# Pooled attention and a routed FFN: scores by key without row maxima, heads in array tiles, FFN rows by indirect DMA

## The chip, the core and the metric

The kernel runs on one core of one Trainium2 chip. The metric is the device time of one launch in microseconds, lower is better. All data is fp32. The engines are TensorE (PE in the rows; its weight loads are PEld), VectorE (DVE), ScalarE (ACT), GpSimd (POOL) and SyncE (SP), which here only issues DMAs.

## The reference

```python
# attention: q, k, v are (8 batches, 8 heads, 1152, 64)
q_pool = q.reshape(B, H, S // 2, 2, D).mean(axis=3)        # 576 queries
scores = (1 / sqrt(D)) * q_pool @ k.transpose(0, 1, 3, 2)
scores = scores - scores.max(axis=-1, keepdims=True)
attn = exp(scores)
attn = attn / (attn.sum(axis=-1, keepdims=True) + 1e-09)
x = (attn @ v) -> (B, 576, 512)                             # heads side by side
# routed FFN, per batch, on the 128 tokens of highest score x @ w_gate
h = maximum(x[top] @ w1, 0)                                 # w1: 512 x 1024
out = x.copy()
out[top] = x[top] + sigmoid(score[top])[:, None] * (h @ w2) # w2: 1024 x 512
```

q, k and v are random numbers of size 0.1.

## The kernel before

Heads go in pairs, 32 pairs in all. `load_pair` (L112) loads a pair on SP: k with 128 partitions of nine rows of 64 numbers each, q, and v with a column of ones beside it. `prepare_pair` (L140) adds each two queries on GpSimd (L144), transposes k and the pooled q on TensorE in 128x128 blocks (L164, L173) and copies them out of PSUM, so that a head's 64 dimensions lie on 64 partitions, head 0 on the first half and head 1 on the second.

The work then runs in steps of one score tile: 128 queries of one head against all 1152 keys, nine steps a pair (four query tiles per head; the ninth holds the last 64 queries of both heads). `scores` (L182) makes three matmuls of 384 columns (L188), queries as the weights. `exponents` (L197) takes row maxima on VectorE (L200), folds them (L202, L203) and runs three exponents on ScalarE with the maximum as bias (L208). `transposed` (L217) turns the attention tile with nine TensorE transposes (L222) and copies each third out (L227 on ScalarE, L229 on VectorE). `weighted` (L233) multiplies by the values (L241): nine chunks, attention as the weights, 65 moving columns, the last of which collects the row sums. `normalized` (L249) divides and writes x.

`advance` (L485) sets the order: the scores of a step, then the transposes of the step before mixed with the values of the one before that. A generator of the next pair's preparation and one of the last batch's FFN are called once a step in between.

`routed` (L273) is that FFN: gate scores from x (L282), a row of all scores by transposes (L307, L315), ranks by comparison (L332, L341, L351), a 0/1 matrix of token against slot (L368), its transposes (L379, L383), the chosen rows by matmul with that matrix (L394), the two FFN layers (L412, L427), and the update spread over all tokens by matmul (L446) and added (L453). x then goes to the output in one piece. The order of instructions is the framework's, by the order of the program and priorities.

Of the kernel before, what the change touches and what calls it, by code (L numbers as in the profile page):

```python
# [9 lines left out]

P = 128
F32 = mybir.dt.float32
I32 = mybir.dt.int32
AF = mybir.ActivationFunctionType
ALU = mybir.AluOpType
AX = mybir.AxisListType


def _rows_of(ap_1d: bass.AP, parts: int) -> bass.AP:
    """The same row for each of `parts` partitions."""  # L20
    return dataclasses.replace(ap_1d, ap=[[0, parts]] + [list(x) for x in ap_1d.ap])


@with_exitstack
def kernel(
    ctx: ExitStack,
# [9 lines left out]
):  # L36
    """Pooled-query attention, two heads at a time, then the routed FFN of a batch while the next
    batch's attention runs.

    Keys: key p * NC + c is row p of chunk c, so a partition's rows of k and v lie together.  # L40
    Tokens: token p * NF + t is row p of tile t < NF; the last TAIL tokens are tile NF. The last
    tiles of a pair's two heads share one score tile, by queries in a block diagonal.
    """
    nc = tc.nc

    B, H, S, D = q.shape
    Sp = S // 2
    Dm = H * D
    F = moe_w1.shape[1]
    NC = S // P  # L50
    NF = Sp // P
    TAIL = Sp - NF * P
    NT = NF + 1
# [3 lines left out]
    G = 3  # L57
# [3 lines left out]
    D1 = D + 1  # L61
    # The mean of two queries is half their sum.
    scale = 0.5 / math.sqrt(D)
# [8 lines left out]
    const = ctx.enter_context(tc.tile_pool(name="const", bufs=1))  # L72
    load = ctx.enter_context(tc.tile_pool(name="load", bufs=2))
    work = ctx.enter_context(tc.tile_pool(name="work", bufs=3))
    small = ctx.enter_context(tc.tile_pool(name="small", bufs=4))
# [8 lines left out]
    make_identity(nc, ident[:, :])  # L84
    # before[p, j] = 1 where j < p
    before = const.tile([P, P], F32, name="before")
    nc.gpsimd.memset(before[:, :], 1.0)
    nc.gpsimd.affine_select(
        out=before[:, :],
        in_=before[:, :],  # L90
        compare_op=ALU.is_gt,
        fill=0.0,
# [16 lines left out]

# [1 line left out]

    def load_pair(b, hp):  # L112
# [16 lines left out]
        )  # L129
        # The column of ones gives the sums of the attention's rows.  # L130
        v_sb = load.tile([P, 2, NC, D1], F32, name="v_sb", bufs=3)
# [8 lines left out]
    def prepare_pair(pair):  # L140
        """kT and qT: head, then dimension, by key or pooled query; a PSUM tile at a time."""
        qp = load.tile([P, NT, 2, D], F32, name="qp")
# [90 lines left out]
    def weighted(step, g, j, at):  # L233
        """Chunks of group g of attention times values, of head j, into column block `at`."""
        v_sb, t = step["pair"]["v"], step["t"]
        rows = P if t < NF else TAIL
        cols = slice(0, P) if t < NF else slice(j * TAIL, (j + 1) * TAIL)
        if g == 0 and at == 0:
            av_tiles["av"] = ps_av.tile([P, NF, D1], F32, name="av")
        for c in range(g * CG, (g + 1) * CG):  # L240
            nc.tensor.matmul(  # L241
                av_tiles["av"][0:rows, at, :],
                lhsT=step["pT"][:, c, cols],
                rhs=v_sb[:, j, c, :],
                start=(c == 0),
                stop=(c == NC - 1),
            )

    def normalized(step):  # L249
        """The finished column blocks, divided by their rows' sums, into x."""  # L250
        x, j, t, hp = step["x"], step["j"], step["t"], step["pair"]["hp"]
# [18 lines left out]

# [1 line left out]

    def routed(b, x):  # L273
        """The FFN of batch b on its `capacity` best tokens, in units to put between steps."""
        tiles = [(t, P if t < NF else TAIL) for t in range(NT)]

        if slots:
# [14 lines left out]
            gate = ffn.tile([P, NT], F32, name="gate")  # L292
            # exp(88) is finite, and 1 / (1 + exp(88)) is nothing beside 1.
            nc.vector.tensor_scalar(
# [7 lines left out]

            # All scores on every partition, bit for bit, by transposing columns repeated.
            sc_row = ffn.tile([P, Sp], F32, name="sc_row")
# [17 lines left out]

            # rank: how many tokens come before, by score, equal scores by position.
            parts = ffn.tile([P, NT, 3], F32, name="rank_parts")
# [39 lines left out]
        for s0, w in slots:  # L364
            # pick[token, slot] = 1 where the token's rank is the slot.
            pick = ffn.tile([P, NT, P], F32, name="pick")
# [101 lines left out]

    # ---- the steps, each one score tile; a step's transposes and its product with the values
    # ---- come one and two steps later, the next pair and the last batch's FFN in between  # L470

# [13 lines left out]
    def advance(now):  # L485
        """The stages of the step before and of the one before that, after `now`'s scores."""
        if now is not None:
# [42 lines left out]


# [1 line left out]
_INS = ["q", "k", "v", "moe_w_gate", "moe_w1", "moe_w2"]  # L533
# [28 lines left out]
```

## Time and profile before

| | |
|---|---|
| time, median of 3 | 1845.32 us (1843.73 to 1845.55) |
| span of the profiled execution | 1838.1 us |
| TensorE / VectorE / ScalarE / GpSimd busy | 1809.5 / 954.7 / 763.1 / 73.1 us |
| chain that ended last | TensorE 98% |
| mean granted TensorE clock | 0.997 |
| DMA | 166,459 packets, 72.42 MB, 39 GB/s over the span |

How to read it: busy time is the union of an engine's instructions; matmuls are pipelined, so their durations overlap and only their pitch tells what one costs. The chain goes back from the last instruction, at each step to what released it; what is not on it costs nothing by itself.

### The profile page before, as it was taken

How to read it: one execution, taken by the hardware profiler on the slowest of the kernel's cores; microseconds unless marked ns; L12 is line 12 of the kernel's file. 1: busy time of each engine (PE TensorE's matmuls, PEld its weight loads, DVE VectorE, ACT ScalarE, POOL GpSimd, SP SyncE). 2: the span in 40 equal slices, each digit the busy share in tenths (PEclk: the TensorE clock that was granted, in tenths of full speed). 3: DMA queues.
4: the chain of work that ended last, by engine and by line, in shares of the span. 5: the costliest groups of instructions: out<-in, count | busy, mean ns of one | idle time of the engine just before them, and what ended most of it. 6: DMA issues, size and time to landing. Idle time of an engine off the chain costs nothing.

```text
span 1838.1 us, 29462 instructions
## 1 busy us (share of the span) xinstructions
PE 1809.5 (98%) x11648; PEld 1359.5 (74%) x11648; DVE 954.7 (52%) x2609; ACT 763.1 (42%) x1545; POOL 73.1 (4%) x201
## 2 busy tenths in 40 slices
PE   8999999999999999999999999999999999999996
PEld 5777777777778677776778777777777867778674
DVE  2355566445663456535664356644566445663451
ACT  2244444334443344434444344443444434443440
POOL 1000000000000000000000000000000000000000
PEclk9999999999999999999999999999999999999998
DMA  8111111112110111102111111111211101100000
GB/s 213 39 39 40 40 39 28 40 27 65 27 39 27 49 42 40 39 14 65 39 30 36 27 52 40 40 27 27 65 32 34 39 27 53 27 14 1 24 4 26
DMA packets 166459, 72.42 MB, mean 39 GB/s; under 512 B 150832, under 2 KB 154928, under 8 KB 165296
## 3 DMA queue, kind: packets, MB, share of 16 engines
q1 hardware_dynamic: 166320, 70.53, 14.9%
q8 instruction: 92, 1.51, 0.3%
q14 instruction: 47, 0.39, 0.1%
HBM read 61.08 MB, written 9.44 MB: 38 GB/s over the span
## 4 chain that ended last, share of the span: by engine, by line
PE 98%; DVE 1%; DMA 0%; ACT 0%; issue 0%; SPq 0%; POOL 0%
PE sc L188 34%; PE av L241 31%; PE tr L222 19%; PE ps L412 3%; PE ps L427 3%; PE ps L394 3%; PE ps L446 2%; PE tr L164 2%; PE tr L173 1%; PE tr L177 0%; DMA q_sb<-in_q_dram 0%; PE ps L379 0%; DVE x L453 0%; DVE gate_prod L282 0%; PE ps L307 0%; DVE cmp L341 0%
## 5 line engine op out<-in xcount | busy, mean ns | idle before, releaser
L241 PE MATMUL av<-v_sb,pT 128*128 128x65 f32 (+1 forms) x5760 | 700.9, 261 | 1.0 <-DVE x L264 1.0
L200 DVE TENSOR_REDUCE top<-sc 128x1 f32<-128x384 f32 x864 | 481.2, 557 | 404.3 <-PE sc L188 358.8
L241 PEld LDWEIGHTS av<-v_sb,pT 128*128 128x128 f32 (+1 forms) x5760 | 662.0, 183 | 25.5 <-issue 24.4
L188 PE MATMUL sc<-kT,qT 64*128 64x384 f32 (+1 forms) x1728 | 656.2, 512 | 1.7 <-ACT p L208 1.3
L227 ACT COPY pT<-tr 128x384 f32<-128x384 f32 x576 | 275.4, 478 | 897.5 <-PE tr L222 894.7
L208 ACT ACTIVATE p<-sc,neg 128x384 f32<-128x384 f32 x864 | 467.9, 581 | 39.8 <-DVE neg L203 22.5
L188 PEld LDWEIGHTS sc<-kT,qT 64*128 64x128 f32 (+1 forms) x1728 | 306.2, 191 | 222.2 <-issue 60.4
L222 PE MATMUL tr<-ident,p 128*128 128x128 f32 x2592 | 452.7, 284 | 0.0
L222 PEld LDWEIGHTS tr<-ident,p 128*128 128x128 f32 x2592 | 305.4, 154 | 159.2 <-issue 144.9
L229 DVE COPY pT<-tr 128x384 f32<-128x384 f32 x288 | 160.6, 558 | 133.9 <-PE tr L222 130.8
L167 DVE COPY kT<-tr 128x384 f32<-128x384 f32 x96 | 53.5, 558 | 88.2 <-PE tr L164 88.1
L144 POOL TENSOR_TENSOR qp<-q_sb 128x256 f32<-128x256 f32 x64 | 45.0, 724 | 1024.1 <-PE tr L177 764.5
L255 DVE TENSOR_SCALAR rec<-av 128x4 f32<-128x4 f32 (+1 forms) x96 | 15.2, 159 | 108.5 <-PE av L241 108.5
L453 DVE SCALAR_TENSOR_TENSOR x<-ps,gate,x 128x512 f32<-128x512 f32 (+1 forms) x40 | 30.0, 749 | 68.0 <-PE ps L446 67.5
L412 PE MATMUL ps<-xeT,w 128*128 128x128 f32 x512 | 63.7, 278 | 1.4 <-ACT hT L421 0.7
L412 PEld LDWEIGHTS ps<-xeT,w 128*128 128x128 f32 x512 | 59.5, 192 | 2.2 <-ACT hT L421 0.9
L427 PE MATMUL ps<-w,hT 128*128 128x512 f32 x128 | 57.5, 593 | 0.7 <-ACT hT L421 0.7
L202 DVE TENSOR_REDUCE neg<-top 128x1 f32<-128x3 f32 x288 | 44.5, 155 | 23.5 <-ACT pT L227 1.4
L164 PE MATMUL tr<-ident,k_sb 128*128 128x128 f32 x288 | 49.6, 284 | 6.5 <-DMA k_sb<-in_k_dram 6.5
L394 PE MATMUL ps<-pick,x 128*128 128x128 f32 (+1 forms) x320 | 50.5, 300 | 0.3 <-ACT pickT L386 0.3
L203 DVE TENSOR_SCALAR neg<-neg 128x1 f32<-128x1 f32 x288 | 43.9, 153 | 8.6 <-DVE neg L202 0.2
L394 PEld LDWEIGHTS ps<-pick,x 128*128 128x128 f32 (+1 forms) x320 | 41.9, 196 | 7.1 <-ACT pickT L386 0.5
(59 smaller groups left out, 447.4 us busy)
## 6 DMA issues: line engine op xcount, KB each, us to landing
k_sb<-in_k_dram SPq DMA_DIRECT2D x64, 288.0 KB, 3.9
v_sb<-in_v_dram SPq DMA_DIRECT2D x64, 288.0 KB, 3.7
q_sb<-in_q_dram SPq DMA_DIRECT2D x32, 512.0 KB, 3.9
out_dram<-x SPq DMA_DIRECT2D x8, 1024.0 KB, 3.9
w<-in_moe_w_dram SPq DMA_DIRECT2D x2, 2048.0 KB, 13.3
q_tail<-in_q_dram SPq DMA_DIRECT2D x32, 64.0 KB, 3.7
out_dram<-x SPq DMA_DIRECT2D x8, 128.0 KB, 2.7
w_gate<-in_moe_w_gate_dram SPq DMA_DIRECT2D x1, 256.0 KB, 7.2
```

Of the source, the lines that this page charges most:

```text
L164: nc.tensor.transpose(tr[:, i * P : (i + 1) * P], pair["k"][:, g * CG + i, :, :], ident[:, :])
L167: nc.vector.tensor_copy(kT[:, g * CG : (g + 1) * CG, :].rearrange("p c n -> p (c n)"), tr[:, 0 : CG * P])
L188: nc.tensor.matmul(sc[:, :], lhsT=pair["qT"][rows, t, :], rhs=pair["kT"][rows, g * CG : (g + 1) * CG, :].rearrange("p c n -> p (c n)"), st ...
L200: nc.vector.tensor_reduce(top[:, g : g + 1], step["sc"][g][:, :], AX.X, ALU.max)
L208: nc.scalar.activation(p[:, g * CG : (g + 1) * CG, :].rearrange("p c n -> p (c n)"), step["sc"][g][:, :], AF.Exp, bias=neg[:, 0:1], scale= ...
L222: nc.tensor.transpose(tr[:, i * P : (i + 1) * P], step["p"][:, g * CG + i, :], ident[:, :])
L227: nc.scalar.copy(to, tr[:, 0 : CG * P])
L229: nc.vector.tensor_copy(to, tr[:, 0 : CG * P])
L241: nc.tensor.matmul(av_tiles["av"][0:rows, at, :], lhsT=step["pT"][:, c, cols], rhs=v_sb[:, j, c, :], start=(c == 0), stop=(c == NC - 1),)
L394: nc.tensor.matmul(pv[:, c, 0:w], lhsT=x[0:rows, t, c * P : (c + 1) * P], rhs=pick[0:rows, t, 0:w], start=(t == 0), stop=(t == NT - 1),)
L412: nc.tensor.matmul(pv[:, f, 0:w], lhsT=w1[:, c, (f0 + f) * P : (f0 + f + 1) * P], rhs=xeT[:, c, 0:w], start=(c == 0), stop=(c == ND - 1),)
L427: nc.tensor.matmul(ps[0:w, 0:Dm], lhsT=hT[:, f, 0:w], rhs=w2[:, f, :], start=(f == 0), stop=(f == NFC - 1),)
```

## The change

The old code stays whole as `_any_scores`, behind a branch at the end of the program (comments are dropped). A new class `_Plain` runs first:

- k and q are loaded by 32-column halves of a head, so that a partition holds a 32x32 block's row (pieces of 128 bytes in DRAM); VectorE transposes the blocks (`prepare_pair`). No transposes of k and q on TensorE.
- Scores are made with keys as the weights and 288 pooled queries (half of the 576) as moving columns, for both heads: head 0 on array rows 0 to 63, head 1 on 64 to 127, into two PSUM banks. ScalarE takes one exponent over both, without a maximum.
- The result is already attention by key, so it is the moving operand of attention times values; v of a head is the weights, 64 columns, head 0 into output partitions 0 to 63 and head 1 into 64 to 127 of one bank.
- Row sums: attention tiles are added up on VectorE, then summed over keys by a matmul with ones (`normalized`). All sums are kept, and the number outside 0.05 to 1e12 is counted at the end (`outside`); if it is not zero, the old code runs after all.
- x is written to a DRAM buffer in pieces of 128 bytes (`finished`); the FFN copies the buffer to the output, finds ranks as before, gathers the 128 chosen rows by an indirect DMA, and writes their results over the output's rows by another.
- The order of instructions is that of the program (`manual_schedule`). A step is a group of three key chunks of a half; six steps a pair. The FFN's units come in two steps out of three.

```diff
+    def load_pair(self, b, hp):
+        kb = self.load.tile([P, self.KB, BLK], F32, name="kb")
+        qb = self.load.tile([P, self.QB, 2, BLK], F32, name="qb")
+        v_sb = self.load.tile([P, 2, self.NC, self.D], F32, name="v_sb", bufs=3)
+        for j, ds, rows in self.quarters():
+            h = 2 * hp + j
+            nc.sync.dma_start(
+                kb[rows, :, :], self.k[b, h, :, ds].rearrange("(n i) d -> i n d", i=BLK)
+            )
+            nc.sync.dma_start(
+                qb[rows, :, :, :].rearrange("i n r d -> i (n r) d"),
+                self.q[b, h, :, ds].rearrange("(i m) d -> i m d", i=BLK),
+            )
...
+    def prepare_pair(self, pair):
+        nc.gpsimd.tensor_tensor(
+            out=qp[:, :, :], in0=pair["q"][:, :, 0, :], in1=pair["q"][:, :, 1, :], op=ALU.add
+        )
...
+        nc.vector.transpose(pair["kT"][:, :], pair["k"].rearrange("p n d -> p (n d)"))
+        nc.vector.transpose(pair["qT"][:, :], qp.rearrange("p n d -> p (n d)"))
+
+    def scores(self, grp):
...
+        for u in range(G):
+            c = grp["g"] * G + u
+            sc = self.ps_sc.tile([P, 2, 512], F32, name="sc")
+            for j in range(2):
+                rows = slice(j * self.D, (j + 1) * self.D)
+                nc.tensor.matmul(
+                    sc[:, j, 0:n],
+                    lhsT=pair["kT"][rows, c * P : (c + 1) * P],
+                    rhs=pair["qT"][rows, qs],
...
+            nc.scalar.activation(grp["p"][:, u, :, :], sc[:, :, 0:n], AF.Exp, scale=self.scale)
+
+    def weighted(self, grp):
+        if grp["g"] == 0:
+            self.av = self.ps_av.tile([P, 512], F32, name="av")
+        for u in range(G):
+            c = grp["g"] * G + u
+            for j in range(2):
+                nc.tensor.matmul(
+                    self.av[j * self.D : (j + 1) * self.D, 0:n],
+                    lhsT=grp["pair"]["v"][:, j, c, :],
+                    rhs=grp["p"][:, u, j, :],
+                    start=(c == 0),
+                    stop=(c == self.NC - 1),
+                )
...
+    def added(self, grp, half):
...
+        nc.vector.tensor_tensor(
+            out=acc[:, :, :],
+            in0=first[:, :, :],
+            in1=grp["p"].rearrange("p u j n -> p u (j n)"),
+            op=ALU.add,
+        )
...
+    def drained(self, half):
+        self.nc.vector.transpose(
+            half["avb"].rearrange("p n d -> p (n d)"), self.av[:, 0 : self.HALF]
+        )
+
+    def normalized(self, half):
...
+            nc.tensor.matmul(
+                ps[j * self.D : (j + 1) * self.D, 0:n],
+                lhsT=self.ones[:, 0 : self.D],
+                rhs=half["sum"][:, j, :],
...
+        nc.vector.transpose(smb.rearrange("p n d -> p (n d)"), ps[:, 0:n])
+
+    def finished(self, half):
...
+            nc.sync.dma_start(
+                half["xs"][:, d0 + ds.start : d0 + ds.stop].rearrange("(i n) d -> i n d", i=BLK),
+                x[rows, hp, :, :],
+            )
+    def routed(self, b, xs, part):
...
+        nc.sync.dma_start(self.out[b], xs[:, :])
...
+            nc.gpsimd.indirect_dma_start(
+                out=xe[0:w, :],
+                in_=xs[:, :],
+                in_offset=bass.IndirectOffsetOnAxis(ap=index[0:w, 0:1], axis=0),
...
+            nc.gpsimd.indirect_dma_start(
+                out=rows_out,
+                out_offset=bass.IndirectOffsetOnAxis(ap=index[0:w, 1:2], axis=0),
+                in_=xe[0:w, :],
+    def run(self):
...
+        for step in range(n_groups + 2):
...
+                self.scores(groups[step])
+            if 1 <= step <= n_groups:
+                self.weighted(groups[step - 1])
+            if step < n_groups:
+                self.added(groups[step], halves[step // self.NG])
+            if step >= 1 and step % self.NG == 0:
+                self.drained(halves[step // self.NG - 1])
+            if step >= self.NG + 1 and step % self.NG == 1:
+                half = halves[step // self.NG - 1]
+                self.normalized(half)
+                if half["s"] == 1:
+                    self.finished(half)
...
+            else:
+                next(routing, None)
+            if step < n_groups and i == 3 and n + 1 < len(pairs):
+                self.prepare_pair(upcoming)
...
+        with tc.manual_schedule():
+            outside = plain.run()
+    with tc.If(outside > 0):
+        _any_scores(tc, *args)
```

`quarters` gives the two heads' two 32-column halves, each with its 32 partitions. In PSUM, score tiles have three buffers of two banks, `av` one bank, and all other TensorE outputs (the sums and the FFN's) one.

## Rows read from the trace of the kernel before

**Rows 1.** The page, busy us, share of the span and instructions of each engine.

```profile
PE 1809.5 (98%) x11648; PEld 1359.5 (74%) x11648; DVE 954.7 (52%) x2609; ACT 763.1 (42%) x1545; POOL 73.1 (4%) x201
```

**Rows 2.** The page, chain that ended last: shares by engine, then by line.

```profile
PE 98%; DVE 1%; DMA 0%; ACT 0%; issue 0%; SPq 0%; POOL 0%
PE sc L188 34%; PE av L241 31%; PE tr L222 19%; PE ps L412 3%; PE ps L427 3%; PE ps L394 3%; PE ps L446 2%; PE tr L164 2%; PE tr L173 1%; PE tr L177 0%; DMA q_sb<-in_q_dram 0%; PE ps L379 0%; DVE x L453 0%; DVE gate_prod L282 0%; PE ps L307 0%; DVE cmp L341 0%
```

**Rows 3.** Groups by form: line, engine, op, tile, shape, count | busy us, mean ns | idle before.

```profile
L188 PE MATMUL sc<-kT,qT 64*128 64x384 f32 x1536 | 584.9, 513 | 1.7 <-ACT p L208 1.3 <-ACT qT L174 0.4
L188 PE MATMUL sc<-kT,qT 128*128 128x384 f32 x192 | 71.3, 509 | 0.0
L200 DVE TENSOR_REDUCE top<-sc 128x1 f32<-128x384 f32 x864 | 481.2, 557 | 404.3 <-PE sc L188 358.8
L222 PE MATMUL tr<-ident,p 128*128 128x128 f32 x2592 | 452.7, 284 | 0.0
L227 ACT COPY pT<-tr 128x384 f32<-128x384 f32 x576 | 275.4, 478 | 897.5 <-PE tr L222 894.7
```

**Rows 4.** Timeline, two stretches: start us, us, engine, line, op, count [idle before <-releaser].

```profile
102.69 1.48 PEld L241 LDWEIGHTS av<-v_sb,pT 128*64 128x64 f32 x24 [0.17 <-issue]
...
845.16 2.10 PE L188 MATMUL sc<-kT,qT 128*128 128x384 f32 x6
847.10 0.49 PE L222 MATMUL tr<-ident,p 128*128 128x128 f32 x3
848.40 1.05 ACT L208 ACTIVATE p<-sc,neg 128x384 f32<-128x384 f32 x2 [0.24 <-DVE neg L203]
849.94 1.08 PE L446 MATMUL ps<-ye,pickT 128*128 128x512 f32 x2
850.95 2.20 PE L188 MATMUL sc<-kT,qT 64*128 64x384 f32 x6
853.08 0.55 PE L222 MATMUL tr<-ident,p 128*128 128x128 f32 x3
```

**Rows 5.** Timeline of the last FFN: w1 units (L412) and w2 (L427).

```profile
1807.90 3.84 PE L412 MATMUL ps<-xeT,w 128*128 128x128 f32 x32 [0.68 <-ACT xeT L403]
...
1816.95 7.13 PE L427 MATMUL ps<-w,hT 128*128 128x512 f32 x16 [0.69 <-ACT hT L421]
```

**Rows 6.** Groups by form, as rows 3: ScalarE copies, VectorE comparisons, GpSimd's add.

```profile
L174 ACT COPY qT<-tr 128x512 f32<-128x512 f32 x32 | 18.7, 585 | 14.4 <-PE tr L173 14.3
L341 DVE TENSOR_SCALAR_CACHE_REDUCE cmp<-sc_row,gate_sc 128x576 f32<-128x576 f32 x8 | 6.4, 805 | 0.0
L341 DVE TENSOR_SCALAR_CACHE_REDUCE cmp<-sc_row,gate_sc 128x192 f32<-128x192 f32 x8 | 3.2, 404 | 0.0
L144 POOL TENSOR_TENSOR qp<-q_sb 128x256 f32<-128x256 f32 x64 | 45.0, 724 | 1024.1 <-PE tr L177 764.5 <-PE ps L315 231.2 <-DMA q_sb<-in_q_dram 28.4
```

**Rows 7.** The page's packets and one issue; a window: length, busy by engine, clock, DMA share, GB/s.

```profile
DMA packets 166459, 72.42 MB, mean 39 GB/s; under 512 B 150832, under 2 KB 154928, under 8 KB 165296
...
k_sb<-in_k_dram SPq DMA_DIRECT2D x64, 288.0 KB, 3.9
...
610.00:611.00 1.00, 1.00 (x3) 0.38 (x2) 0.00 (x0) 0.00 (x0) 0.00 (x0) 1.00 1.04 237
```

**Rows 8.** Timeline of TensorE early on, and a window there (clock: third number from the end).

```profile
11.48 5.49 PE L188 MATMUL sc<-kT,qT 64*128 64x384 f32 x8 [0.38 <-ACT qT L174]
...
55.32 4.21 PE L188 MATMUL sc<-kT,qT 64*128 64x384 f32 x6
...
86.43 3.81 PE L188 MATMUL sc<-kT,qT 128*128 128x384 f32 x6
93.02 2.20 PE L188 MATMUL sc<-kT,qT 64*128 64x384 f32 x6
...
55.00:60.00 5.00, 5.00 (x11) 2.38 (x10) 2.11 (x4) 0.00 (x0) 0.00 (x0) 1.00 0.00 0
```

**Rows 9.** A window of the tail, columns as in rows 7.

```profile
1780.00:1838.10 58.10, 38.48 (x231) 27.38 (x229) 17.25 (x64) 7.51 (x16) 0.00 (x0) 0.91 0.05 21
```

More of the change, by code (lines that the diff above doesn't have):

```diff
@@ L11 @@
 P = 128
+BLK = 32
+G = 3
 F32 = mybir.dt.float32
@@ L24, with _any_scores @@
 @with_exitstack
-def kernel(
+def _any_scores(
     ctx: ExitStack,
@@ new lines, with kernel @@
+@with_exitstack
+def kernel(
+    ctx: ExitStack,
+    tc: tile.TileContext,
+    q: bass.AP,
+    k: bass.AP,
+    v: bass.AP,
+    moe_w_gate: bass.AP,
+    moe_w1: bass.AP,
+    moe_w2: bass.AP,
+    capacity: int,
+    out: bass.AP,
+):
+    args = (q, k, v, moe_w_gate, moe_w1, moe_w2, capacity, out)
+    if capacity % P == 1:
+        _any_scores(tc, *args)
+        return
+    with ExitStack() as stack:
+        plain = _Plain(stack, tc, *args)
+        with tc.manual_schedule():
+            outside = plain.run()
+    with tc.If(outside > 0):
+        _any_scores(tc, *args)
```

401 lines of the change are left out of this document (added).

## The prediction

> **What bounds the kernel now.** I read the busy table first [rows 1]: TensorE has work for 1809.5 of 1838.1 us, VectorE for 954.7, ScalarE for 763.1, GpSimd for 73.1. "Busy" alone proves little, so the chain of waits comes next [rows 2]: 98% of the chain that ended last lies on TensorE, and its three large shares are the score matmuls (L188, 34%), attention times values (L241, 31%) and the transposes of attention (L222, 19%). So time falls only with TensorE's work, until another engine or the DMA is late.
>
> The groups by form [rows 3] give that work. A matmul here is two passes, each with its own weight load: 864 score tiles stand as 1536 + 192 passes. A 64-row pass of 384 columns takes as long as a 128-row one (513 and 509 ns with the pipeline's ends): half the rows idle is not half the time. The timeline [rows 4] gives the pitch behind these means. At 845.16 six 128-row score passes start and the next transposes follow at 847.10: 1.94 / 6 = 0.323 us per 384 columns, 0.84 ns a column.
>
> **What the change removes.** All 2592 transposes of attention, the row maxima (481.2 us of VectorE), the copies of transposed attention (275.4 us of ScalarE for two groups in three, the third on VectorE) and the transposes of k and q on TensorE [rows 3]; in the routed FFN the pick matmuls (L394) and the scattering ones (L446).
>
> **What TensorE then has.** A pair of heads is six steps (two halves of 288 queries, three groups of three key chunks), 192 steps in all. A step has 3 chunks x 2 heads x 2 passes of scores and as many of attention times values, each of 288 columns: 288 x 0.84 = 0.242 us. A weight load of 128 columns can come every 0.12 us (32 passes in 3.84 [rows 5]), one of 64 columns every 0.06 (24 in 1.48 us [rows 4]), so both hide under 0.242.
>
> One question carries the sum: the two heads of a chunk use different rows of the array (scores, 64x128) or different columns (values, 128x64). Does TensorE run them at the same time?
> - One after the other: 24 x 0.242 = 5.81 us a step.
> - Side by side: passes start in program order (head 0 first, head 0 second, head 1 first, head 1 second), so head 1's first pass runs beside head 0's second, and its second beside the next chunk's first. 12 passes take 7 places instead of 12: 2 x 7 x 0.242 = 3.39 us.
>
> No row of before shows two tiles at once: there every row-tiled score tile of a step is on the same head. The serial rows are nearer in form; yet I take side by side, since within a pair of tiles nothing is shared that the rows show as a cost: other array cells, other input partitions, other output banks or partitions. Both ends stay in the range. The Trainium skill (TensorEngine Tiling (Array Packing), "Tiling Modes") says that different tiles can execute weight loads and matmuls in parallel; no run here shows it, and by it alone a step would be the 3.39 us.
>
> Each step changes tile form twice. That has a price in the timeline [rows 4]: from the start of L446's two passes at 849.94 to the 64-row scores at 850.95 is 1.01 us, where two passes of 512 columns are 0.86, so 0.15 going in; and the six 64-row passes hold the next transposes for 853.08 - 850.95 = 2.13 us instead of 1.94, 0.19 going out. Together 0.34 a step. So a step is 3.73 us, and 192 of them 716 us.
>
> Beside that:
> - the sums of the rows by a matmul with ones, 4 passes in 3 places per half, 0.73 us x 64 = 47 us;
> - the FFN of a batch: two w1 units of 3.84 us, w2 of 7.13 less its end, 6.9 [rows 5]; four transposes of the gathered rows 0.6; the gate scores' row 1.0; columns, index matmuls 1.5; eight units that each change tile form once more, 8 x 0.17 = 1.4; sum 19.1. Seven batches run it between steps: 134 us. The eighth is in the tail.
>
> **Who could be late.** ScalarE: 576 exponents of 576 columns. Two of 384 take 1.05 us [rows 4], and copies of 512 and 384 columns differ by 107 ns [rows 6], 0.84 ns a column, so 0.525 + 192 x 0.00084 = 0.69 us, 395 us in all and 2.1 per step of 3.73: hidden, and the score tiles have three buffers. If TensorE is serial, hidden still more.
>
> VectorE: comparisons of 576 and 192 columns take 805 and 404 ns [rows 6], so 1.04 ns a column and 0.2 fixed. Per pair: four adds of 1728 columns, 2.0 us each; four of 576, 0.81; two drains, two transposes of sums and two products of 288, 0.5 each; small ones 0.64; k and q in 32x32 blocks (1152 and 576 columns) and the gate's reduction, 3.0: 17.9 us. No row shows a 32x32 transpose; I take a column per cycle like the others, with twice that as the bad end (+3.2 us a pair, still under TensorE's 22). Times 32 is 573; the FFN adds about 12 a batch, 667 us in all. Hidden on average. Not always: the one output bank `av` waits for its drain, which stands on VectorE behind the adds and, in some steps, behind a rank unit of 3 us. I charge 20 us, bounds 0 and 100.
>
> GpSimd: an add of 256 columns takes 724 ns [rows 6], so 576 about 1.6 us, two per pair, hidden. The gather and the scatter of rows by indirect DMA have no row; a gather has two empty units (over 7 us) to land, against 3.9 us from issue to landing of a plain load [rows 7], so I charge it only in the tail.
>
> DMA: k and q now come in pieces of 128 bytes, x goes to DRAM in such pieces. Per pair: k 4608, q 4608, v 2304 of 256 bytes, x 2304: 13,824 packets, 442,000 in all against 166,459 now. While the queues were full of 256-byte packets they moved 237 GB/s [rows 7], 0.93 packets per ns. At that rate a pair needs 14.9 us, of about 28 that it lasts. Loads are issued nearly a pair ahead; on SP they stand behind the writes of x and, once a batch, the copy of 1.2 MB to the output, some 10 us. Hidden, until packets come at under half that rate. A page of the Trainium skill speaks against this part: DMA: Bandwidth & Descriptors, "Specifications", asks for at least 512 bytes, below which a transfer reads, modifies and writes. The trace's 256-byte loads show no such loss at 237 GB/s; for stores it shows nothing, and if only the 2304 stores cost double, the pair needs 17.3 us, still hidden.
>
> **Start and tail.** Before, the first scores start at 11.5 us [rows 8]. Now 9216 packets of k and q come first (9.9 us at that rate, with 0.8 to the first issue and 2 to land), then GpSimd's add and the block transposes: 16 us. TensorE's clock starts low: at 55.32 six score passes take 4.21 us, at 93.02 the same six take 2.20 [rows 8], the first at 1.2 GHz, the second at 2.4, though the granted clock is shown as 1.00 there. What came just before was the first step of 128-row scores (86.43); 64-row steps had gone on since 11.5 with TensorE hardly idle. Side by side the array is filled as by those, so I charge 20 us; if it stayed low until the first FFN, about 110.
>
> Tail: from 1780 on before has 58.1 us [rows 9]. The new one has no scattering matmuls, but writes x to DRAM, gathers, and scatters (three transfers of about 4 us), and at the end reads the check's count and branches on every engine. The low clock can come in it as it did (0.91 on the mean of those 58.1 us). I take 68.
>
> Sum: 16 + 20 + 716 + 47 + 134 + 20 + 68 = 1021 us of span. The profiled execution of before, 1838.1, stands 7.2 below the median of 1845.3, so 1028: I say **1030**. Its own range is 900 (no empty places, no stalls) to 1150 (clock late).
>
> **Rivals.**
> - Only one of the two tile kinds runs side by side: five more places of 0.242 per step, 1.21 x 192 = 232 us: 1260. For it: nothing says that rows and columns behave alike.
> - Neither does: 464 + 15 for the sums: 1510, up to 1700 if the clock stays low to the first FFN. For it: every row of before is serial. Against it: as above.
> - The DMA binds: at 40 ns a packet per engine instead of 17, a pair takes 34.6 us, 1110 + 85 for start and tail: 1200. Before's packets speak against it, their size for it.
> - Slower than before: neither kind overlaps and half-filled passes keep the clock at 1.2 GHz, as they did from 11.5 to 86 us. All of TensorE's 1311 us is doubled: 2820. It decides from the point where over a quarter of that work (335 us) runs at the low clock. Against it: 64-row scores in the middle of before did not bring the clock down.
> - The change does not do what it says: a sum outside its bounds sends the whole old code after the new: 2880. q and k are 0.1 in size, so exponents are near 1 and each sum near 1152, within 0.05 and 1e12.
>
> **How the numbers follow.** Side by side 0.62; one kind 0.12; neither 0.12; DMA or VectorE in the way (1150 to 1500) 0.06; slower by the clock 0.07; by the branch 0.01. The range 900 to 1520 takes in the first, the second, most of the DMA case and half of the third: over 0.8. A measurement tells this kernel from no change at about 0.2%. All cases but the last two are faster: 0.91; within 0.2%: 0.01; slower 0.08.
>
> **What would show it.** Score passes of the two heads that start within a few ns of each other in pairs, a step of 3.7 us, VectorE near 65% and DMA packets near 442,000 show the steps right. A step of 5 or 6.2 us shows a rival; score passes 0.48 us apart show the clock; TensorE waiting on v, k or q shows the DMA, and waiting on `av` VectorE.

## The result, and the profile after

The changed kernel takes 951.93 us (median of 4 runs, 951.33 to 953.0) against 1844.53 us for the kernel before (1842.5 to 1845.55): ratio 0.5176, 95% interval 0.5145 to 0.5207. The forecast was 1030 us, so the way was right and the size 8% too high. The profiled execution spans 949.5 us.

The page of the changed kernel: busy us, share of the span and instructions; the granted TensorE clock in 40 slices (tenths of full speed); packets; the chain that ended last.

```profile
PE 844.1 (89%) x5695; PEld 500.2 (53%) x5695; DVE 629.0 (66%) x1069; ACT 359.5 (38%) x625; POOL 109.4 (12%) x91
...
PEclk9999998999999999999999999899998999989958
...
DMA packets 453419, 84.97 MB, mean 89 GB/s; under 512 B 450528, under 2 KB 450528, under 8 KB 453088
...
issue 39%; PE 27%; DVE 18%; SPq 5%; POOL 5%; DMA 4%; ACT 2%; POOLq 0%; DVEq 0%
```

Beside [rows 1] TensorE has fallen from 1809.5 to 844.1 us, and its 98% of the chain [rows 2] has become 27%, with VectorE at 18%: TensorE still has the most work, but it now waits for others too. The 39% of "issue" is time for which this view names no releaser; one piece of it, 24.05 us, stands ahead of GpSimd's product at 474.05, and TensorE was at work in most of it. So these shares are a hint only, and the waits below carry the reading. The clock has 8s in the middle, and 5 and 8 at the end.

The timeline of TensorE in a stretch without disturbance: start us, us, engine, line, op, count.

```profile
434.73 1.73 PE L710 MATMUL sc<-qT,kT 64*128 64x288 f32 x12
...
437.99 1.73 PE L710 MATMUL sc<-qT,kT 64*128 64x288 f32 x12
439.64 1.68 PE L727 MATMUL av<-p,v_sb 128*64 128x288 f32 x12
441.25 1.73 PE L710 MATMUL sc<-qT,kT 64*128 64x288 f32 x12
...
444.41 0.66 PE L770 MATMUL ps<-sum,ones 128*64 128x288 f32 x4
445.00 1.73 PE L710 MATMUL sc<-qT,kT 64*128 64x288 f32 x12
```

From 437.99 to 441.25 a step takes 3.26 us, where 3.73 were forecast. A half of three steps takes 445.00 - 434.73 = 10.27 us, so the sums cost 0.49 of it. Twelve passes take 1.63 us on the mean: six places of 0.242 and some 0.18 for the form switch. In the trace's single records the passes of the two heads start 6 to 8 ns apart, from the very first pair of a phase.

The waits of TensorE from 19 to 890 us: for what, us in total, times, longest us.

```profile
PE av L727 <- DVE avb L760: 22.7, 10, 2.9
PE ps L926 <- DVE pick L916: 19.9, 7, 3.7
PE ps L842 <- DVE diag L830: 19.6, 7, 2.8
```

All 62.2 us are for VectorE. What stands in its queue is seen at one of them. The timeline of VectorE there:

```profile
448.63 0.75 DVE L809 TENSOR_REDUCE part<-prod 128x18 f32<-128x576 f32 x1 [1.52 <-POOL prod L803]
449.30 2.48 DVE L745 TENSOR_TENSOR acc<-acc,p 128x1728 f32<-128x1728 f32 x1
451.81 0.76 DVE L755 TENSOR_TENSOR sum<-acc 128x576 f32<-128x576 f32 x1
452.61 0.76 DVE L756 TENSOR_TENSOR sum<-sum,acc 128x576 f32<-128x576 f32 x1
453.28 0.27 DVE L826 TENSOR_REDUCE line<-part 128x18 f32<-128x72 f32 x1
453.58 0.76 DVE L830 TENSOR_TENSOR diag<-line,same 128x576 f32<-128x576 f32 x1
454.26 0.47 DVE L760 STREAM_TRANSPOSE avb<-av 128x288 f32<-128x288 f32 x1
```

and of TensorE over the same stretch, then two windows (length, TensorE's busy time, granted clock, DMA share, GB/s):

```profile
454.39 1.17 PE L842 MATMUL ps<-diag,ones 128*128 128x288 f32 x2 [2.80 <-DVE diag L830]
455.49 2.95 PE L710 MATMUL sc<-qT,kT 64*128 64x288 f32 x12
...
456.00:458.00 2.00, 2.00 (x10) 0.50 0.94 145
458.00:462.00 4.00, 4.00 (x32) 1.00 1.35 144
```

The score row's matmuls (L842) come in a step that closes a half. `diag` for them is queued behind the last add of the half and its two closing sums, so TensorE stands 2.80 us. Not all of that queue is work: VectorE itself stood 1.52 us for GpSimd's product ahead of it (L809; 48.7 us in 32 such places), and the add took 2.48 us in place of 1.96 (see the last section). No run moved that reduction. TensorE then works at a granted clock of 0.50 (1.2 GHz) until 458: the scores take 2.95 us instead of 1.73. This wait is paid twice. Over all half-microsecond windows of 19 to 893 us such stretches add up to 68 us at 0.50, of which half, 34 us, is lost.

The time by terms, from these rows:

| term | forecast | measured |
|---|---|---|
| to the first scores | 16 | 14.4 |
| low clock at the start | 20 | 1.4 |
| 192 steps | 716 | 3.26 x 192 = 626 |
| sums | 47 | 0.49 x 64 = 31 |
| seven FFN between steps | 134 | 127 |
| stalls | 20 | 62 of waits + 34 of low clock |
| tail | 68 | 53.8 |
| sum | 1021 | 950 |

The FFN stands by its units in the trace (two of 3.77, one of 7.07 and small ones, 18.1 a batch), the tail from the last product of attention (895.7) to the end. The sum is the span of 949.5 within 1 us.

### The profile page after: what moved, and what is told of

It is laid out like the page before. It is cut to its first block, busy times and chain, and to the rows that moved or that the text cites. A ratio compares the mean times of both kernels' runs of the same rounds, so it can differ in the third digit from the quotient of the medians.

```text
span 949.5 us, 14253 instructions
## 1 busy us (share of the span) xinstructions
PE 844.1 (89%) x5695; PEld 500.2 (53%) x5695; DVE 629.0 (66%) x1069; ACT 359.5 (38%) x625; POOL 109.4 (12%) x91
## 2 busy tenths in 40 slices
DMA packets 453419, 84.97 MB, mean 89 GB/s; under 512 B 450528, under 2 KB 450528, under 8 KB 453088
## 4 chain that ended last, share of the span: by engine, by line
issue 39%; PE 27%; DVE 18%; SPq 5%; POOL 5%; DMA 4%; ACT 2%; POOLq 0%; DVEq 0%
PE sc L710 9%; PE av L727 8%; DVE acc L745 6%; PE ps L965 6%; DMA qb<-in_q_dram 3%; POOL qp L692 3%; SPq L675 2%; SPq L798 2%; DVE cmp L889 2%; PE ps L977 1%; SPq L678 1%; ACT p L717 1%; DVE sum L755 1%; POOL prod L803 1%; PE ps L926 1%
## 5 line engine op out<-in xcount | busy, mean ns | idle before, releaser
L717 ACT ACTIVATE p<-sc 128x576 f32<-128x576 f32 x576 | 336.1, 651 | 408.3 <-PE sc L710 389.6
L710 PE MATMUL sc<-qT,kT 64*128 64x288 f32 x2304 | 352.3, 438 | 9.9 <-DVE qT L698 9.9
L727 PE MATMUL av<-p,v_sb 128*64 128x288 f32 x2304 | 332.2, 425 | 22.7 <-DVE avb L760 22.7
L710 PEld LDWEIGHTS sc<-qT,kT 64*128 64x128 f32 x2304 | 221.0, 195 | 124.3 <-issue 71.8
L727 PEld LDWEIGHTS av<-p,v_sb 128*64 128x64 f32 x2304 | 152.3, 140 | 181.7 <-issue 77.1
L745 DVE TENSOR_TENSOR acc<-p 128x1728 f32<-128x1728 f32 x64 | 124.6, 1947 | 115.4 <-ACT p L717 115.1
L745 DVE TENSOR_TENSOR acc<-acc,p 128x1728 f32<-128x1728 f32 x64 | 137.0, 2141 | 10.0 <-ACT p L717 9.5
L803 POOL TENSOR_TENSOR prod<-x,w_gate 128x576 f32<-128x576 f32 x32 | 44.9, 1403 | 568.9 <-DVE x L786 568.9
L809 DVE TENSOR_REDUCE part<-prod 128x18 f32<-128x576 f32 x32 | 24.1, 753 | 48.7 <-POOL prod L803 48.7
L755 DVE TENSOR_TENSOR sum<-acc 128x576 f32<-128x576 f32 x64 | 49.6, 775 | 2.2
L756 DVE TENSOR_TENSOR sum<-sum,acc 128x576 f32<-128x576 f32 x64 | 49.6, 775 | 2.2
L692 POOL TENSOR_TENSOR qp<-qb 128x576 f32<-128x576 f32 x32 | 45.9, 1435 | 22.8 <-DMA qb<-in_q_dram 22.6
L697 DVE STREAM_TRANSPOSE kT<-kb 128x1152 f32<-128x1152 f32 x32 | 43.0, 1345 | 6.2 <-DMA kb<-in_k_dram 6.2
L770 PE MATMUL ps<-sum,ones 128*64 128x288 f32 x256 | 42.7, 413 | 1.5 <-DVE sum L756 1.5
## 6 DMA issues: line engine op xcount, KB each, us to landing
w<-in_moe_w_dram SPq DMA_DIRECT2D x2, 2048.0 KB, 11.1
```

The lines of the kernel that those rows point to most:

```text
L692: nc.gpsimd.tensor_tensor(out=qp[:, :, :], in0=pair["q"][:, :, 0, :], in1=pair["q"][:, :, 1, :], op=ALU.add)
L697: nc.vector.transpose(pair["kT"][:, :], pair["k"].rearrange("p n d -> p (n d)"))
L710: nc.tensor.matmul(sc[:, j, 0:n], lhsT=pair["kT"][rows, c * P : (c + 1) * P], rhs=pair["qT"][rows, qs], start=True, stop=True,)
L717: nc.scalar.activation(grp["p"][:, u, :, :], sc[:, :, 0:n], AF.Exp, scale=self.scale)
L727: nc.tensor.matmul(self.av[j * self.D : (j + 1) * self.D, 0:n], lhsT=grp["pair"]["v"][:, j, c, :], rhs=grp["p"][:, u, j, :], start=(c == 0 ...
L745: nc.vector.tensor_tensor(out=acc[:, :, :], in0=first[:, :, :], in1=grp["p"].rearrange("p u j n -> p u (j n)"), op=ALU.add,)
```

## The experiments

All times are medians; each ratio is to the kernel before on the same chip. Changes of a term are taken between the profiled spans.

| kernel | us | ratio, 95% interval |
|---|---|---|
| after | 951.93 | 0.5176, 0.5145 to 0.5207 |
| e1_heads_in_turn | 1093.33 | 0.5938, 0.5921 to 0.5955 |
| e2_same_rows | 1147.36 | 0.6231, 0.6202 to 0.6261 |
| e3_no_ranks | 905.73 | 0.4919, 0.4905 to 0.4933 |
| e4_big_loads | 948.28 | 0.515, 0.5135 to 0.5165 |
| e5_even_units | 887.45 | 0.4829, 0.4794 to 0.4864 |
| e6_gpsimd_sums | 927.82 | 0.5051, 0.5014 to 0.5088 |
| e7_both | 917.89 | 0.4994, 0.4958 to 0.503 |
| e8_drain_first | 893.83 | 0.4851, 0.4841 to 0.4861 |

### Do the two heads run side by side? e2_same_rows

```diff
-                rows = slice(j * self.D, (j + 1) * self.D)
+                rows = slice(0, self.D)
```

> Both score matmuls of a chunk use head 0's rows of the array and head 0's data; head 1's scores are left out (head 0's are computed twice). Counts, columns and output banks stay. Theory overlap (two heads in two row tiles run side by side, which halves the time of a phase): 12 places instead of 6 in the score phase, 6 x 0.242 = 1.45 us a step, 192 steps, +279: 1225 to 1240 us, and the score passes start 0.24 us apart, one at a time. Rival (the gain is from fewer and longer passes alone): about 952 us.

The timeline of TensorE in this kernel, and a window (length, its busy time, clock, DMA share, GB/s):

```profile
449.96 3.17 PE L710 MATMUL sc<-qT,kT 64*128 64x288 f32 x12
453.06 1.68 PE L727 MATMUL av<-p,v_sb 128*64 128x288 f32 x12
454.67 3.17 PE L710 MATMUL sc<-qT,kT 64*128 64x288 f32 x12
...
335.67 1.36 PE L926 MATMUL ps<-meta,pick 128*128 128x3 f32 x10
...
339.00:345.00 6.00, 6.00 (x21) 0.50 0.16 44
```

The same twelve passes in the same array rows take 3.10 us, the products beside them still 1.61. A step is 454.67 - 449.96 = 4.71 us, 1.45 more: six places of 0.242. That shows the pairing. Over 192 steps it is 278 us; the span grew by only 194. The rest came back: VectorE has more time in each step, so no wait of TensorE is left in the middle (-62), and 14 us of low clock stand there instead of 68 (-27). So 278 - 89 = 189. The time is below the expected 1225 to 1240 us, because the expectation left out what comes back; the cost of the step is the expected one. The rival (no overlap) would have left the time where it was. The 14 us of low clock are two stretches, and no wait of TensorE stands before them: each begins behind the ten passes with `pick`, of three columns (the row at 335.67 and the window behind it show one).

### How far ahead may the second tile start? e1_heads_in_turn

Same passes, but all of head 0's ahead of all of head 1's, in both phases:

```diff
...
-        for u in range(G):
-            c = grp["g"] * G + u
-            for j in range(2):
+        for j in range(2):
+            for u in range(G):
+                c = grp["g"] * G + u
```

> In each step all three score matmuls of head 0 come first in the program, then all three of head 1; attention times values likewise. Nothing is left out. Theory A (the matmuls of the two array tiles wait in queues of their own, so that head 1 starts beside head 0 wherever it stands near in the program): 6 places of 0.242 us per phase as in the changed kernel, about 952 us, within 15. Theory B (matmuls start in program order, and only neighbours in different tiles overlap): 11 places instead of 6 per phase, 5 x 0.242 x 2 = 2.42 us a step, 192 steps, +464: about 1415 us.

Neither was met. The timeline of TensorE:

```profile
454.68 2.21 PE L730 MATMUL av<-p,v_sb 128*64 128x288 f32 x12
456.82 2.31 PE L710 MATMUL sc<-qT,kT 64*128 64x288 f32 x12
459.07 2.21 PE L730 MATMUL av<-p,v_sb 128*64 128x288 f32 x12
```

A phase is 2.2 us: neither six places (1.6) nor theory B's eleven (2.8), but about 8.5. The single records show how. Head 0's passes go alone at a pitch of 0.242 us; head 1's first weight load is issued 0.595 us after head 0's first, from there both run side by side until head 0 is through, and head 1's last passes stand alone. Head 1's first pass starts 5 to 6 ns after head 0's third, in both phases. So a matmul started ahead of the three later passes of the other tile that stand before it in the program, not ahead of all six. A step is 459.07 - 454.68 = 4.39 us, 1.13 longer, 217 us in all; waits fell by 53 and the low clock's loss by 26, which leaves 138, and 141 were measured. Program order is a part of the price, then, and the change's order (heads alternating) is the one that has no empty place.

### Is it a queue on VectorE? e3_no_ranks

The ranking by comparison is left out:

```diff
-        rank = ffn.tile([P, NT], F32, name="rank")
-        for t, rows in tiles:
...
-        nc.vector.tensor_reduce(rank[:, :], parts[:, :, :], AX.X, ALU.add)
+        rank = self.token
```

> The ranking is left out: the first 128 tokens are taken instead of the best, everything else stays. VectorE loses about 8 us a batch. Theory queue (TensorE's waits in the middle, about 70 us for the gate row, the drain of the output bank and the picks, come from VectorE's FFN units that stand in front of what TensorE needs, and these waits bring its clock down afterwards): the waits on the drain fall from 22.7 us to under 10, those on the picks from 27 to under 10, the low clock gets rarer, and with some 8 us less in the tail the time is 890 to 915 us. Rival (VectorE is late by its mean load of 66%, whatever stands where): under 15 us gained beyond the 8 of the tail, 930 to 945 us.

The waits of TensorE in the middle of this kernel:

```profile
PE ps L842 <- DVE diag L830: 19.7, 7, 2.8
PE ps L888 <- DVE pick L878: 11.0, 7, 1.6
PE av L727 <- DVE avb L760: 4.6, 8, 0.6
```

VectorE has 46.6 us less work (582.4 busy), and the span is 45.4 us shorter; the time lies between the first theory's bounds. The waits behind which rank units stood fell (avb 22.7 to 4.6, pick 19.9 to 11.0), the one with no rank unit ahead of it, `diag`, stayed at 19.7. With 14 us less lost to the low clock these are 41 of the 45 us; the rest lies in the tail, where the ranks are left out too (48.4 us from the last product of attention, against 53.8). It speaks for the queue; yet VectorE's load fell as well, so it does not yet tell order from load.

### Order or load? e5_even_units and e6_gpsimd_sums

e5 leaves all work on its engine and moves only the FFN's units: VectorE's go into steps that close no half, a unit of TensorE comes a step later than the VectorE unit that it reads, and ranks are cut into units of one token tile. In the code a unit marked "d" (VectorE's) may come in the first two steps of a half, one marked "p" (TensorE's) in the first and the last, one marked "e" in any.

```diff
...
-            if t % 2 == 1:
-                yield
+            if t < NT - 1:
+                yield "d"
...
-            else:
-                next(routing, None)
+                        self.kind = "d"
+            g = step % self.NG
+            if self.kind == "e" or g == 0 or g == (1 if self.kind == "d" else 2):
+                self.kind = next(routing, "e")
```

> The same work in another order: the FFN's units that VectorE works (gate row, one token tile's ranks each, picks) are cut smaller and put only into the steps in which VectorE does not close a half's sums; the units of TensorE that wait for them come a step later. No instruction is left out or added. Theory queue (TensorE waits because of where VectorE's units stand): its waits on the gate row, the bank's drain and the picks, 62 us between 19 and 890, fall under 15, the low clock in the middle (68 us of it) gets rare, and the time is 865 to 890 us. Rival (VectorE's mean load): VectorE has the same 629 us of work, so 935 us or more.

e6 leaves the order and takes VectorE's closing sums to GpSimd:

```diff
-        nc.vector.tensor_tensor(out=to, in0=acc[:, 0, :], in1=acc[:, 1, :], op=ALU.add)
-        nc.vector.tensor_tensor(out=to, in0=to, in1=acc[:, 2, :], op=ALU.add)
+        nc.gpsimd.tensor_tensor(out=to, in0=acc[:, 0, :], in1=acc[:, 1, :], op=ALU.add)
+        nc.gpsimd.tensor_tensor(out=to, in0=to, in1=acc[:, 2, :], op=ALU.add)
```

> The two adds of 576 columns that close a half (99 us of VectorE) move to GpSimd, where an add of that size takes 1.4 us. Rival of e5 (mean load): VectorE falls from 629 to about 530 us, and TensorE's waits and the low clock fall with it: 895 to 920 us. Theory queue alone: the drain waits less, but the gate row and the picks stay as they are: 925 to 945 us. If GpSimd's adds come late behind its waits for the gather, or slow VectorE's own, over 945 us.

e5: engines, TensorE's longest waits from 19 us on, and a window of the middle (length, TensorE's busy time, clock, DMA share, GB/s).

```profile
PE 812.9 (92%) x5695; PEld 482.4 (55%) x5695; DVE 616.7 (70%) x1069; ACT 356.8 (40%) x625; POOL 109.6 (12%) x91
...
PE av L727 <- DVE avb L760: 29.9, 30, 1.5
...
19.00:830.00 811.00, 781.04 (x5559) 1.00 0.66 99
```

e6: engines, and TensorE's waits in the middle.

```profile
PE 829.5 (90%) x5695; PEld 492.9 (53%) x5695; DVE 545.1 (59%) x941; ACT 358.6 (39%) x625; POOL 291.0 (31%) x219
...
PE ps L926 <- DVE pick L916: 25.6, 7, 3.7
PE ps L842 <- DVE diag L830: 13.3, 7, 2.0
PE av L727 <- DVE avb L760: 12.0, 7, 1.7
```

With VectorE's work all but unchanged (616.7 against 629.0 us) e5 saved 64.4 us of span: the waits for `diag` and `pick` are gone, avb's came in 30 short pieces, and the granted clock is 1.00 over 811 us, where the changed kernel lost 34 us. 32 us of waits and 34 of clock are 66. The time is within the queue theory's bounds; the waits are not, 29.9 us where under 15 were expected. With 84 us less work on VectorE e6 saved 25: waits fell by 11, clock loss by 15, and the wait for `pick` even grew from 19.9 to 25.6; its time is in the bounds of the queue alone. So order made the larger part of the stalls: it alone took away 64 of their 96 us. Over a third of that price (34 of 96 us) is what the clock takes behind the waits. Which of e5's three moves did how much was not taken apart, and the 30 us that stay are another matter (e7 and e8). By the terms e5's sum is 14.4 + 1.4 + 626 + 31 + 127 + 30 + 53 = 883 of a span of 885.1: next to nothing is unexplained there. (The 53 count from 832 on, since the last unit of the seventh FFN runs behind the last product of attention in e5.) It is the lowest time of this study.

### Both together: e7_both

The two edits above in one kernel.

```diff
-        nc.vector.tensor_tensor(out=to, in0=acc[:, 0, :], in1=acc[:, 1, :], op=ALU.add)
+        nc.gpsimd.tensor_tensor(out=to, in0=acc[:, 0, :], in1=acc[:, 1, :], op=ALU.add)
...
+            if self.kind == "e" or g == 0 or g == (1 if self.kind == "d" else 2):
+                self.kind = next(routing, "e")
```

> e5 and e6 together. If placing alone removes the waits, the same as e5 within 10 us; if load counts beside it, 10 to 25 us less than e5. Floor from the changed kernel's own rows: 14.4 start + 626 for steps + 37 sums + 127 FFN + 54 tail = 858 us of span.

A miss: 30 us over e5. TensorE's largest wait, and one place of it in the timelines of GpSimd, VectorE and TensorE:

```profile
PE ps L770 <- POOL sum L756: 26.0, 15, 2.7
...
147.67 3.20 POOL L756 TENSOR_TENSOR sum<-sum,acc 128x576 f32<-128x576 f32 x1
147.67 1.95 DVE L745 TENSOR_TENSOR acc<-p 128x1728 f32<-128x1728 f32 x1
150.93 0.71 PE L770 MATMUL ps<-sum,ones 128*64 128x288 f32 x4 [2.70 <-POOL sum L756]
```

Seven of the 15 waits, 18.9 of the 26.0 us, are like the one shown: GpSimd's second sum starts at the same moment as an add of VectorE and takes 3.20 us in place of 1.41, and the matmul with ones (L770) waits 2.70 us for it. Seven more are of 0.97 us, behind sums of the usual length. The gather in the same queue, which the expectation of e6 had named as a risk, makes none of these waits. The waits for avb fell to 3.4 us as they did not in e5: with the sums off VectorE, its queue ahead of the drain is short enough. But with the 26.0 us came 11.1 more for the transpose of the row sums (`smb`), and 17 us of clock loss that e5 does not have: 10.6 us of waits more in all, and 17 of clock, of 31 us of span. The queue was moved, not removed.

### The rest of e5's waits: e8_drain_first

```diff
-        if grp["g"] < self.NG - 1:
-            return
+    def closed(self, half):
...
                 self.drained(halves[step // self.NG - 1])
+                self.closed(halves[step // self.NG - 1])
```

> e5_even_units with one more move: the two closing sums (L755, L756; 0.76 us each) are issued on VectorE behind the transpose that drains the accumulators (L760), no longer ahead of it. Nothing is left out. Theory (the 30 us of short waits of TensorE for that transpose that e5 still has are a queue behind the two sums): the waits fall under 10 us and the time is 860 to 872 us; the sums are then needed 1.5 us later, by the ones matmuls, and some of the gain may come back as a wait there. Rival (the waits are VectorE's load in a half of three steps, 9 us and more of work in some 10.4 us, whatever the order): the waits move to the ones matmuls (L770) or to the scores' readers and the time stays within 880 to 892 us.

A miss as well, and 2 us above the rival's bound too. The waits of TensorE, one of the new ones, and VectorE's rows ahead of it, then the same two rows of VectorE in e5:

```profile
PE av L727 <- DVE avb L761: 21.2, 21, 1.3
PE ps L929 <- DVE smb L779: 8.1, 7, 1.2
...
482.13 1.25 PE L929 MATMUL ps<-meta,pick 128*128 128x3 f32 x9 [1.16 <-DVE smb L779]
...
483.36 2.95 PE L710 MATMUL sc<-qT,kT 64*128 64x288 f32 x11
...
473.15 1.95 DVE L745 TENSOR_TENSOR acc<-acc,p 128x1728 f32<-128x1728 f32 x1
...
481.61 0.46 DVE L779 STREAM_TRANSPOSE smb<-ps 128x288 f32<-128x288 f32 x1
...
470.17 1.95 DVE L745 TENSOR_TENSOR acc<-acc,p 128x1728 f32<-128x1728 f32 x1
...
478.75 0.47 DVE L778 STREAM_TRANSPOSE smb<-ps 128x288 f32<-128x288 f32 x1
```

The closing sums were a third of that queue: the drain now follows the big add at once, but this add itself starts late behind rank units, so 21.2 of 29.9 us stay. TensorE, held up less there, then meets VectorE's queue a step later: the transpose of the row sums (L779) still has to read the only bank of its pool, into which the matmuls with `pick` (L929) want to write, 8.1 us of new waits. The swap does not delay that transpose: from the add to it VectorE works without a pause, 8.46 us in e8 and 8.58 in e5, on the same work. So in these steps VectorE's load is the limit and the wait only moved, as the rival says and as e7's short waits for avb bear out. Five stretches at 0.50 lose another 8.5. 8.7 saved and 16.6 paid make 7.9, and the span is 7.8 us over e5's (the intervals of the two ratios overlap).

### Are the small loads hidden? e4_big_loads

k and q are loaded in pieces of 4608 bytes instead of 128.

```diff
-                kb[rows, :, :], self.k[b, h, :, ds].rearrange("(n i) d -> i n d", i=BLK)
+                kb[rows, :, :].rearrange("i n d -> i (n d)"),
+                self.k[b, h, ds.start * 18 : ds.start * 18 + 576, :].rearrange(
+                    "(i m) d -> i (m d)", i=BLK
+                ),
...
```

> k and q are loaded in pieces of 4608 bytes instead of 128, the same bytes into the same tiles; their layout, and so the scores, are wrong. Packets fall from 453,000 to about 160,000. Theory hidden (loads are issued a pair ahead): the start gains up to 5 us, the rest nothing: 942 to 953 us. Rival (small pieces slow the steady part through late loads or through queues that the gather, the writes of x and the copy share): 900 to 935 us.

```profile
DMA packets 166699, 84.97 MB, mean 90 GB/s; under 512 B 155616, under 2 KB 155616, under 8 KB 166368
```

The page of this kernel has 37% of the packets, and the time fell by 0.4% (948.28 against 951.93; the intervals overlap), within the expected 942 to 953. The first scores start at 10.73 us instead of 14.36, and that is nearly all of the 3.9 us by which the span is shorter. Behind the start the loads were hidden. The stores of x, still in pieces of 128 bytes, were not tried apart.

## Why the prediction was right, and where its sizes were off

**Side by side** was the step that carried the sum, and it held: e2 shows that the second head's passes cost nothing while they stand in other rows, and 1.45 us a step when they do not. The Trainium skill (TensorEngine Tiling (Array Packing), "Tiling Modes") says that different tiles can run weight loads and matmuls in parallel; the pairs in this trace agree, and e1 adds that the order of issue matters. That the two column tiles of the values pair up too is read from their starts and from 1.61 us for twelve passes; no run put both into the same columns.

**The step, 716 forecast and 626 measured**, is the largest mis-sized term. Its pitch (0.242 us) and its switches (0.34 forecast, 0.36 measured) were right. What failed is "passes start in program order ... 12 passes take 7 places instead of 12": head 1's first pass does not wait for head 0's second, the two start together, and 12 passes take 6. That is 0.48 us a step, 93 us; longer switches took 3 of them back. The sums had the same error (3 places charged for 4 passes), 16 us.

**The low clock at the start** was charged at 20 us and cost 1.4: the first 24 score passes took 4.74 us (14.36 to 19.10) instead of 3.3, and from there the pitch is the full one. The reason given, that the array is filled as by 128-row scores, fits that; no run took it apart.

**The stalls** are the term that was too small: 20 forecast, 0 to 100 as bounds, 96 measured. The place was right ("the one output bank `av` waits for its drain, which stands on VectorE behind the adds"), and two things were missing. The FFN's own matmuls wait in the same queue for `diag` and `pick` (39.5 of the 62 us). And the clock goes down behind most of these waits, where the prediction had charged a low clock at the start and in the tail only; e5 shows both gone with the order alone, and 29.9 us of waits for the drain left.

**VectorE, ScalarE, GpSimd** held:

```profile
L697 DVE STREAM_TRANSPOSE kT<-kb 128x1152 f32<-128x1152 f32 x32 | 43.0, 1345 | 6.2 <-DMA kb<-in_k_dram 6.2
L717 ACT ACTIVATE p<-sc 128x576 f32<-128x576 f32 x576 | 336.1, 651 | 408.3 <-PE sc L710 389.6
L803 POOL TENSOR_TENSOR prod<-x,w_gate 128x576 f32<-128x576 f32 x32 | 44.9, 1403 | 568.9 <-DVE x L786 568.9
```

In these groups of after (as [rows 6]) a 32x32 transpose of 1152 columns takes 1345 ns, 1.17 ns a column, so the near one of the two ends was right. An exponent is 651 ns where 690 were charged, GpSimd's operation 1403 where 1600 were. VectorE's total was forecast as 667 us and is 629.0.

**The DMA** held: 453,419 packets (442,000 for the pairs were forecast), and the loads of k and q hidden, as e4 shows. The indirect DMAs, which had no row before, take a median of 3.5 us (gather) and 4.4 us (scatter) to land, and their issue some 1.05 us of GpSimd.

**The tail** was charged at 68 and is 53.8, at a mean clock of 0.68. The prediction adds up no terms for the 68, so which part was too dear stays open; of the three transfers of "about 4 us", the gather (TensorE waits 4.08 us for it) and the scatter (4.4 us to land) were not.

So the total came within 8% in part by luck, because the errors went both ways: 90 + 16 + 20 + 14 + 7 us too much for steps, sums, the start with its clock, tail and FFN, and 76 too little for stalls. Of the rivals none came about; "one kind" and "neither" are excluded by the 3.26 us of a step, the DMA by e4, the low clock throughout by the full pitch from 19.1 us on, the branch by the time.

## What to carry to other kernels

Once the largest engine's work is halved, the order in the queues of the others can decide: place their bulk work in steps in which the next matmul waits for nothing behind it, and let its readers come a step later; here that was worth 64 us with no work removed, and taking work off the same engine in the old order was worth 25. What is left then is load, and a swap within the queue only moves the wait (e8). Issue the passes of two array tiles alternately. Read a wait of the matmul engine together with the clock behind it: here the second price was half of the first.

## What the runs showed of the hardware that was not expected

- Passes in two array tiles pair up from the first one (6 to 8 ns apart), and a later matmul can start ahead of three earlier passes of the other tile (e1).
- In the changed kernel, waits of TensorE of 2.0 to 3.7 us in the middle are, most of them, followed by stretches at a granted clock of 0.50, 3.4 to 6.8 us long; e5, whose longest wait there is 1.5 us until the last batch, has none. A shorter wait did it where the passes with `pick`, of three columns, come right behind it: all five stretches of e8 follow a wait of 1.16 us and nine such passes (1.25 us; there are seven such places). e5 has the same passes with no wait ahead of them and keeps its clock; e2 has them without a wait as well, and in two of seven places the clock falls behind them. What tells these two from the other five stays open.
- VectorE and GpSimd can hold each other up: the second add of a half has two lengths, and in e7 GpSimd's second sum has, too (1.41 and 3.20 us, shown there).

The add's group in the changed kernel (durations in ns, min/median/max, then first and last start), and from its timeline GpSimd's row beside the add at 449.30 shown above:

```profile
L745 DVE TENSOR_TENSOR acc<-acc,p x64: 1947/1958/2481, 23.3 to 893.5; 128x1728 f32<-128x1728 f32 x64
...
448.56 1.40 POOL L692 TENSOR_TENSOR qp<-qb 128x576 f32<-128x576 f32 x1
```

The add starts at 449.30 while GpSimd's runs until 449.96, and takes 2.48 us instead of 1.96. 23 of the 64 are such, each begun while that operation of GpSimd runs, some 12 us in all, and they are a part of the queue above; e6 has none of them, e5 has 8. The Trainium skill (SBUF — State Buffer, "SBUF: two separate sides") tells of one port pair that the two engines take for a whole instruction, against operations of VectorE with two SBUF inputs; the 0.52 us more stand beside the 0.66 us that GpSimd's add still had to run. No run took this apart.
